# Grouped-query softmax attention on one core: per-head PV in the last twelve pairs, Q transposed as 4-byte words, V loaded five pairs behind K

## The chip, the core and the metric

The kernel runs on one core of a Trainium2 chip. A core has five engines, each with its own instruction stream: TensorE (PE, the matrix multiplier; PEld in the profile is its loading of weights), VectorE (DVE), ScalarE (ACT), GpSimd (POOL) and SyncE (SP, which here only issues transfers). Sixteen DMA engines move data between HBM and the on-chip memory SBUF; PE writes to a second on-chip memory, PSUM. The metric is device time in microseconds (us), the median of several runs. The profile is of one further execution.

## The reference, cut to what matters

```python
B, Hq, Hkv, Sq, Sk, D = 16, 32, 8, 16, 2048, 128      # bf16 inputs
k = jnp.repeat(k, 4, axis=1); v = jnp.repeat(v, 4, axis=1)
scores = jnp.einsum("bhqd,bhkd->bhqk", q, k) * D ** -0.5
p = softmax(scores, axis=-1)
return jnp.einsum("bhqk,bhkd->bhqd", p, v)
```

Four query heads with 16 positions each share one K and one V of 2048 x 128, so that each of the 16 x 8 = 128 (batch, KV head) groups has 64 query rows.

## The kernel before

**Pairs.** Two groups make a pair, p = 0 to 63: 128 query rows on the 128 partitions, head 0 on rows 0 to 63 and head 1 on rows 64 to 127. A pair needs 1 MB of K and 1 MB of V. All loops are unrolled; each engine runs its list of operations in program order, and semaphores tie the lists together.

**Transfers (SP, L166 to L210).** For t = 0, 1, ... SP issues K of pair t, the Q of eight pairs where one is due (256 KB), V of pair t - VLAG, and the store of the output of pair t - 12 (32 KB). K has 6 buffers: K of pair p waits until VectorE has transposed K of p - 6 (L171). V has 8 buffers: V of p waits until PE is done with V of p - 8 (L177). V of the last pair, 63, comes as two halves, each with its own semaphore (L182 to L185). All go through one queue and are carried out in the order of issue.

**One pair's way through the engines:**

- VectorE transposes K of the pair in two instructions (L308, function kt). They move blocks of 4-byte words, so that two neighbouring bf16 stay together; the two of a word (called e) lie at a stride of 4 bytes afterwards. The 128 elements of a head are thus handled as four quarters of 32: half b, parity e.
- PE multiplies Q with K (the "S" operation, L261 and L217): 32 matmuls over 32 rows and 512 columns, four of them side by side, into the four PSUM banks S_ps. One S_ps serves all pairs, so S of pair p + 1 waits until VectorE has read S of pair p (L245).
- VectorE scales S into Sneg in SBUF and takes the row minimum of the negated scores (L324).
- ScalarE takes the exponential into P, in bf16, with the row sums (L354). P is laid out so that pairs of bf16 make 4-byte words.
- PE transposes P as 4-byte words, 8 transposes of 128 x 128 in two halves ("PT", L273) into two of three PSUM staging banks ST_ps; ScalarE copies each half to PT in SBUF (L364). In what follows this is called a copy of P.
- PE multiplies P with V ("PV"), three pairs late (PVLAG): for pairs 0 to 60 as 16 matmuls with 128 weight columns, both heads' P, against 256 columns, both heads' V (L289). Half of the result, one head's P with the other's V, is not used. For the last three pairs as 32 matmuls with 64 weight columns against 128 (L295), one for each head, into columns of S_ps that are free by then. The loop over j (16 blocks of 128 keys) is the same in both.
- ScalarE divides by the row sums and writes the output tile ("norm"): two instructions for pairs 0 to 60, since the two useful quarters of O_ps lie apart (L377), one for the last three (L381). PV of the next pair waits for it, as O_ps is used by all (L283); the last three wait for S of pair 63 having been read instead (L281).

**Q.** GpSimd copies the Q of eight pairs (a chunk, c = 0 to 7) into Q4 with each half of a row four times, once for each group of 32 partitions (L161). Then come four "Q parts" (i = 0 to 3) for each chunk: PE transposes into a staging bank ("QT", L239), ScalarE copies it to QT in SBUF ("qe", L344). Before the change, part i is the quarter (b, e): 8 transposes of bf16 at a stride of 4 bytes, 128 columns each. The parts of chunk 0 come at the start; those of chunk c + 1 come in the pairs p with p mod 8 = 2 to 5 of chunk c, one in each, after PT (L125 to L127). So 28 pairs carry a Q part, the last of them pair 53; the document calls them Q pairs.

**The order.** It is written out by hand (L115 to L137). In round p PE does S(p + 1), PV(p - 3), PT(p), and QT in a Q pair. ScalarE does exp(p), norm(p - 3), the two copies of P, and qe in a Q pair. VectorE does Sneg(p), the reciprocal of the row sums of p - 1, and the transposes of K of p + 2. At the end PE does, after S(63): PV(59), PT(62), PV(60), PV(61), PV(62), PT(63), PV(63). ScalarE does, after exp(62): norm(59), the copies of P of 62, exp(63), norm(60), norm(61), norm(62), the copies of P of 63, norm(63).

Of the kernel before, what the change touches and what calls it, by code (L numbers as in the profile page):

```python
# [5 lines left out]
ACT = mybir.ActivationFunctionType  # L6
# [9 lines left out]
NO = 8  # L16
NQ = 2
NSTAGE = 3
VLAG = 4
PVLAG = 3  # L20
SLAG = 12
QLEAD = 7


def bass_standalone__gqa_softmax__sampling_kernel(
# [26 lines left out]
    KT = [sb(f"KT{i}", [128, 2 * J * 64], F32) for i in range(NKT)]  # L52
    Qn = [sb(f"Qn{i}", [128, 8, 128], BF16) for i in range(NQ)]
    Q4 = sb("Q4", [128, 8, 2, 4, 64], BF16)
    QT = [sb(f"QT{i}", [128, 4, 1024], BF16) for i in range(2)]
    Sneg = [sb(f"Sneg{i}", [128, Sk], F32) for i in range(2)]
    P = [sb(f"P{i}", [128, Sk // 2], F32) for i in range(2)]
    PT = [sb(f"PT{i}", [128, J // 2, 128], F32) for i in range(NPT)]
# [83 lines left out]
        return ST_ps[:, 512 * (u % NSTAGE):512 * (u % NSTAGE + 1)]  # L142

    def o_ap(p):
        x = p - (NP - 3)
        return S_ps[:, 512 * x:512 * x + 128]

    with nc.Block() as block:
# [63 lines left out]
        @block.tensor  # L212
        def _(pe):
            pe.wait_ge(sem_id, 3)

            def matmul_on_loaded(out, lhsT, rhs, tile, start, stop):
                return pe.add_instruction(mybir.InstMatmult(  # L217
                    name=nc.get_next_instruction_name(), engine=mybir.EngineType.PE,
                    ins=[pe.lower_ap(rhs), pe.lower_ap(lhsT, for_matmul_weights=True)],
                    outs=[pe.lower_ap(out)],  # L220
                    start_tensor_calc=start, stop_tensor_calc=stop,
                    tile_size=(32, 64), tile_position=tile, ldweights=False,
                ))

            def free(u):
                if u >= NSTAGE:
                    pe.wait_ge(sem_ev, u - NSTAGE + 1)

            for op in pe_prog:
                if op[0] == "QT":  # L230
                    _, c, i, u = op
                    if i == 0:
                        pe.wait_ge(sem_q4, c + 1)
                    free(u)
                    dst = stage_ap(u).bitcast(BF16)
                    src = Q4[:, :, :, :, :].rearrange("p j b r (c e) -> p j b e (r c)", e=2)
                    b, e = divmod(i, 2)
                    for j in range(8):
                        ins = pe.transpose(dst[:, 128 * j:128 * (j + 1)], src[:, j, b, e, :], ident[:, :])  # L239
                    ins.then_inc(sem_st, 1)  # L240
                elif op[0] == "S":
                    _, p = op
                    pe.wait_ge(sem_kt, 2 * p + 2)
                    if p >= 1:
                        pe.wait_ge(sem_max, p)  # L245
                    c, i = divmod(p, 8)
                    if i == 0:
                        pe.wait_ge(sem_ev, last_q[c, 3] + 1)
                    kt = KT[p % NKT][:, :].bitcast(BF16).rearrange("p (t b y e) -> p b e t y", t=J // 2, b=2, e=2)
                    qt = QT[c % 2]  # L250
                    for acc in range(4):
                        b, e = divmod(acc, 2)
                        for u in range(2):
                            for r in range(4):
                                rows = slice(32 * r, 32 * (r + 1))
                                g, h = divmod(r, 2)
                                s_ap = S_ps[64 * g:64 * (g + 1), 512 * (2 * h + u):512 * (2 * h + u + 1)]
                                w = qt[rows, acc, 128 * i + 64 * g:128 * i + 64 * (g + 1)]
                                x = kt[rows, b, e, 4 * u:4 * (u + 1), :]
                                if u == 0:  # L260
                                    ins = pe.matmul(s_ap, w, x, start=(acc == 0), stop=(acc == 3))  # L261
                                else:
                                    ins = matmul_on_loaded(s_ap, w, x, (32 * r, 64 * g), acc == 0, acc == 3)
                    ins.then_inc(sem_s, 1)
                elif op[0] == "PT":
                    _, p, h, u = op
                    if h == 0:
                        pe.wait_ge(sem_exp, p + 1)
                    free(u)
                    dst = stage_ap(u)  # L270
                    for t in range(4):
                        x = 4 * h + t
                        ins = pe.transpose(dst[:, 128 * t:128 * (t + 1)], P[p % 2][:, 128 * x:128 * (x + 1)], ident4[:, :])  # L273
                    ins.then_inc(sem_st, 1)
                elif op[0] == "PV":
                    _, p = op
                    pe.wait_ge(sem_ev, last_p[p, 1] + 1)
                    if p < NP - 1:
                        pe.wait_ge(sem_v[p % NV], 16 * (p // NV + 1))
                    if p >= NP - 3:  # L280
                        pe.wait_ge(sem_max, NP)  # L281
                    elif p >= 1:
                        pe.wait_ge(sem_nm, p)  # L283
                    pt = PT[p % NPT][:, :, :].bitcast(BF16).rearrange("p t (q e) -> p t e q", e=2)
                    for j in range(J):
                        if p == NP - 1 and j % 8 == 0:
                            pe.wait_ge(sem_vl[j // 8], 16)
                        if p < NP - 3:
                            ins = pe.matmul(  # L289
                                O_ps[:, 0:256], pt[:, j // 2, j % 2, :], Vb[p % NV][:, :, j, :],  # L290
                                start=(j == 0), stop=(j == J - 1),
                            )
                            continue
                        for g in range(2):
                            ins = pe.matmul(  # L295
                                o_ap(p)[64 * g:64 * (g + 1), :],
                                pt[:, j // 2, j % 2, 64 * g:64 * (g + 1)],
                                Vb[p % NV][:, g, j, :],
                                start=(j == 0), stop=(j == J - 1),
                                skip_group_check=True,  # L300
                            )
                    ins.then_inc(sem_pv, 1)
# [34 lines left out]
        def _(act):  # L337
            for op in act_prog:
                if op[0] == "qe":
                    _, c, i, u = op  # L340
                    act.wait_ge(sem_st, u + 1)
                    if c >= 2 and i == 0:
                        act.wait_ge(sem_s, 8 * (c - 1))
                    act.activation(  # L344
                        QT[c % 2][:, i, :].rearrange("p (a j) -> p a j", j=8),
                        stage_ap(u).bitcast(BF16).rearrange("p (j a) -> p a j", j=8), ACT.Copy,
                    ).then_inc(sem_ev, 1)
                elif op[0] == "exp":
                    _, p = op
                    act.wait_ge(sem_max, p + 1)  # L350
                    if p >= 2:
                        act.wait_ge(sem_st, last_p[p - 2, 1] + 1)

                    act.activation(  # L354
                        P[p % 2][:, :].bitcast(BF16).rearrange("p (n y e) -> p n y e", n=16, e=2),
                        Sneg[p % 2][:, :].rearrange("p (n e y) -> p n y e", n=16, e=2), ACT.Exp,
                        bias=nbias[:, p:p + 1], scale=-1.0, accum_out=rowsum[:, p:p + 1],
                    ).then_inc(sem_exp, 1)
                elif op[0] == "pe":
                    _, p, h, u = op  # L360
                    act.wait_ge(sem_st, u + 1)
                    if h == 0 and p >= NPT:
                        act.wait_ge(sem_pv, p - NPT + 1)
                    act.activation(  # L364
                        PT[p % NPT][:, 4 * h:4 * (h + 1), :].rearrange("p t q -> p (t q)"),
                        stage_ap(u), ACT.Copy,
                    ).then_inc(sem_ev, 1)
                else:
                    _, p = op
                    act.wait_ge(sem_pv, p + 1)  # L370
                    act.wait_ge(sem_rec, p + 1)
                    if p >= NO:
                        act.wait_ge(sem_o[p % NO], 16 * (p // NO))
                    if p < NP - 3:
                        for g in range(2):
                            rows = slice(64 * g, 64 * (g + 1))
                            ins = act.activation(Osb[p % NO][rows, :], O_ps[rows, 128 * g:128 * (g + 1)], ACT.Copy,  # L377
                                                 scale=rrec[rows, p:p + 1])
                        ins.then_inc(sem_nm, 1)
                        continue  # L380
                    act.activation(Osb[p % NO][:, :], o_ap(p), ACT.Copy,  # L381
                                   scale=rrec[:, p:p + 1]).then_inc(sem_nm, 1)
# [28 lines left out]
```

## Time and profile before

| | |
|---|---|
| time, median of 3 runs (lowest, highest) | 348.14 us (347.62, 348.2) |
| the profiled execution: its own time | 348.5 us |
| its span, first to last instruction | 346.7 us |
| PE, ACT, DVE busy | 93%, 89%, 86% of the span |
| moved | 138.94 MB, 401 GB/s over the span |
| granted TensorE clock, mean | 0.995 |

The profile's page has the busy share of each engine, the span in 40 slices (8.67 us each here), the chain of work that ended last, and groups of instructions: line, engine, operation, output and inputs, shape, count, then busy time, mean ns of one, and the idle time ahead of them with what ended it. Besides the page, the trace answers with a timeline of instructions (start, us, engine, line), with who waited for whom, and with the time from the issue of a transfer to its landing. A matmul's busy time holds its way through the array; how fast matmuls follow each other is read from their starts. Times below are counted from the start of the span.

### The profile page before, as it was taken

The page shows a single profiled execution, that of the slowest core. Times are in us where ns is not written, and L with a number is a line of the kernel's source. Part 1 is how long each engine was busy: PE and PEld are TensorE (multiplying, and loading weights), DVE is VectorE, ACT ScalarE, POOL GpSimd, SP SyncE. Part 2 cuts the span into 40 slices and gives each one's busy share as a digit, 9 for nine tenths or more (in the row PEclk, how much of TensorE's full clock was granted, in tenths as well). Part 3 has the DMA queues.
Part 4 walks back from the last instruction along what each step waited for, and adds up shares of the span by engine and source line. Part 5 has one row for each costly group of instructions (what it writes and reads, how often), then busy time and mean ns, then how long its engine had stood idle before and what let it go on. Part 6 is the DMA issues. An engine that isn't in the chain of part 4 may idle for free.

```text
span 346.7 us, 8194 instructions
## 1 busy us (share of the span) xinstructions
PE 323.0 (93%) x3888; PEld 196.1 (57%) x2864; DVE 297.2 (86%) x320; ACT 308.7 (89%) x414; POOL 30.3 (9%) x15
## 2 busy tenths in 40 slices
PE   0667999999999999999999999999999999999995
PEld 0423565556555655665655565566566556555564
DVE  2279988998899989998989988999899989899950
ACT  1438999999999999999999999999999999999995
POOL 4500003000300004000040003000040000000000
PEclk9989999999999999999999999999999999999999
DMA  7999999999999999999999999999999999999981
GB/s 297 425 421 414 409 416 412 413 418 416 412 419 414 416 416 414 416 419 420 410 415 416 419 416 413 418 416 416 413 418 415 418 413 417 417 416 416 412 320 31
DMA packets 37300, 138.94 MB, mean 401 GB/s; under 512 B 11408, under 2 KB 11408, under 8 KB 29072
## 3 DMA queue, kind: packets, MB, share of 16 engines
q1 hardware_dynamic: 37264, 138.42, 98.6%
q8 instruction: 27, 0.44, 0.5%
q14 instruction: 9, 0.07, 0.1%
HBM read 136.31 MB, written 2.10 MB: 399 GB/s over the span
## 4 chain that ended last, share of the span: by engine, by line
PE 67%; ACT 21%; issue 6%; DVE 2%; DMA 2%; POOL 1%; ACTq 0%; SPq 0%
PE O_ps L289 25%; PE S_ps L261 15%; PE ST_ps L273 13%; PE S_ps L217 13%; ACT P L354 11%; ACT QT L344 5%; ACT PT L364 3%; PE ST_ps L239 2%; ACT O L377 2%; DMA Qn<-in_q_dram 2%; DVE KT L308 1%; POOL Q L161 1%; DVE Sneg L324 1%; PE S_ps L295 0%; ACT O L381 0%
## 5 line engine op out<-in xcount | busy, mean ns | idle before, releaser
L324 DVE TENSOR_SCALAR_CACHE_REDUCE Sneg<-S_ps 128x2048 f32<-128x2048 f32 x64 | 146.6, 2290 | 33.1 <-PE S_ps L217 32.0
L354 ACT ACTIVATE P<-Sneg,nbias 128x2048 bf16<-128x2048 f32 x64 | 158.7, 2479 | 7.7 <-DVE Sneg L324 6.1
L308 DVE STREAM_TRANSPOSE KT<-Kn 128x1024 f32<-128x1024 f32 x128 | 150.6, 1216 | 6.6 <-DMA Kn<-in_k_dram 6.6
L289 PEld LDWEIGHTS O_ps<-Vb,PT 128*128 128x128 bf16 x976 | 90.6, 98 | 49.2 <-issue 21.8
L289 PE MATMUL O_ps<-Vb,PT 128*128 128x256 bf16 x976 | 117.2, 273 | 0.0
L261 PE MATMUL S_ps<-KT,QT 32*64 32x512 bf16 x1024 | 103.5, 392 | 5.8 <-DVE Sneg L324 4.4
L217 PE MATMUL S_ps<-KT,QT 32*64 32x512 bf16 x1024 | 102.2, 387 | 0.0
L364 ACT ACTIVATE PT<-ST_ps 128x512 f32<-128x512 f32 x128 | 69.6, 595 | 5.1 <-PE ST_ps L273 3.0
L273 PE MATMUL ST_ps<-ident,P 128*128 128x128 f32 x512 | 69.9, 280 | 4.0 <-ACT P L354 2.9
L261 PEld LDWEIGHTS S_ps<-KT,QT 32*64 32x64 bf16 x1024 | 29.6, 103 | 69.0 <-issue 57.3
L273 PEld LDWEIGHTS ST_ps<-ident,P 128*128 128x128 f32 x512 | 55.9, 142 | 17.6 <-ACT P L354 16.4
L377 ACT ACTIVATE O<-O_ps,rrec 64x128 bf16<-64x128 f32 x122 | 44.1, 361 | 11.7 <-PE O_ps L289 10.1
L161 POOL COPY Q<-Qn 128x4096 bf16<-128x4096 bf16 x8 | 28.8, 3600 | 226.9 <-PE ST_ps L239 222.6
L344 ACT ACTIVATE QT<-ST_ps 128x1024 bf16<-128x1024 bf16 x32 | 32.7, 1032 | 9.3 <-PE ST_ps L239 9.3
L239 PE MATMUL ST_ps<-ident,Q 128*128 128x128 bf16 x256 | 20.6, 231 | 10.2 <-POOL Q L161 10.2
L239 PEld LDWEIGHTS ST_ps<-ident,Q 128*128 128x128 bf16 x256 | 18.2, 104 | 10.5 <-issue 10.2
L315 DVE RECIPROCAL rrec<-rowsum 128x1 f32<-128x1 f32 x64 | 10.1, 158 | 3.9 <-ACT P L354 3.9
L354 ACT ACTIVATION_READ_ACCUMULATOR P<-Sneg,nbias 128x1 f32 x64 | 12.1, 189 | 0.0
L324 DVE DVE_READ_ACCUMULATOR Sneg<-S_ps 128x1 f32 x64 | 5.3, 83 | 0.0
L295 PE MATMUL S_ps<-Vb,PT 128*64 128x128 bf16 x96 | 3.1, 220 | 1.0 <-ACT PT L364 1.0
L295 PEld LDWEIGHTS S_ps<-Vb,PT 128*64 128x64 bf16 x96 | 2.7, 110 | 1.5 <-ACT PT L364 1.3
L381 ACT ACTIVATE O<-S_ps,rrec 128x128 bf16<-128x128 f32 x3 | 1.0, 365 | 1.2 <-PE S_ps L295 1.2
(8 smaller groups left out, 3.0 us busy)
## 6 DMA issues: line engine op xcount, KB each, us to landing
Kn<-in_k_dram SPq DMA_DIRECT2D x64, 1024.0 KB, 16.0
Vb<-in_v_dram SPq DMA_DIRECT2D x63, 1024.0 KB, 17.9
Qn<-in_q_dram SPq DMA_DIRECT2D x8, 256.0 KB, 15.5
out_dram<-O SPq DMA_DIRECT2D x64, 32.0 KB, 15.9
Vb<-in_v_dram SPq DMA_DIRECT2D x2, 512.0 KB, 12.3
```

Source lines behind the costliest of these rows:

```text
L161: gp.tensor_copy(Q4[:, :, :, :, :].rearrange("p j b r x -> p (j b) r x"), src.unsqueeze(2).to_broadcast([128, 16, 4, 64]),).then_inc(sem_q ...
L217: return pe.add_instruction(mybir.InstMatmult(name=nc.get_next_instruction_name(), engine=mybir.EngineType.PE, ins=[pe.lower_ap(rhs), pe.l ...
L239: ins = pe.transpose(dst[:, 128 * j:128 * (j + 1)], src[:, j, b, e, :], ident[:, :])
L261: ins = pe.matmul(s_ap, w, x, start=(acc == 0), stop=(acc == 3))
L273: ins = pe.transpose(dst[:, 128 * t:128 * (t + 1)], P[p % 2][:, 128 * x:128 * (x + 1)], ident4[:, :])
L289: ins = pe.matmul(O_ps[:, 0:256], pt[:, j // 2, j % 2, :], Vb[p % NV][:, :, j, :], start=(j == 0), stop=(j == J - 1),)
L308: dve.transpose(KT[p % NKT][:, :].rearrange("p (t b e a x) -> p x e t b a", t=J // 2, b=2, e=2, x=2)[:, x, :, :, :, :], Kn[p % NK][:, :].b ...
L324: dve.tensor_scalar(Sneg[p % 2][:, :].rearrange("p (t h x) -> p h t x", t=8, h=2), S_ps[:, :].rearrange("p (h t x) -> p h t x", t=8, h=2), ...
L344: act.activation(QT[c % 2][:, i, :].rearrange("p (a j) -> p a j", j=8), stage_ap(u).bitcast(BF16).rearrange("p (j a) -> p a j", j=8), ACT. ...
L354: act.activation(P[p % 2][:, :].bitcast(BF16).rearrange("p (n y e) -> p n y e", n=16, e=2), Sneg[p % 2][:, :].rearrange("p (n e y) -> p n ...
L364: act.activation(PT[p % NPT][:, 4 * h:4 * (h + 1), :].rearrange("p t q -> p (t q)"), stage_ap(u), ACT.Copy,).then_inc(sem_ev, 1)
L377: ins = act.activation(Osb[p % NO][rows, :], O_ps[rows, 128 * g:128 * (g + 1)], ACT.Copy, scale=rrec[rows, p:p + 1])
```

## The change

Three edits. VLAG goes from 4 to 5: V of pair t - 5 is issued behind K of pair t. The Q parts become (half b, half x of the eight pairs): 4 transposes of 4-byte words instead of 8 of bf16, one copy of 128 x 512 4-byte words instead of 128 x 1024 bf16; QT then holds words, and S reads its weights from it at a stride of 4 bytes. And the form of PV with 32 narrow matmuls and one norm instruction starts at pair NP - 12 = 52 instead of 61; pairs 52 to 60 write it to O_ps, the last three to S_ps as before.

```diff
-VLAG = 4
+VLAG = 5
+NFAST = 12
...
-    QT = [sb(f"QT{i}", [128, 4, 1024], BF16) for i in range(2)]
+    QT = [sb(f"QT{i}", [128, 2, 1024], F32) for i in range(2)]
...
     def o_ap(p):
+        if p < NP - 3:
+            return O_ps[:, 0:128]
...
-                    dst = stage_ap(u).bitcast(BF16)
-                    src = Q4[:, :, :, :, :].rearrange("p j b r (c e) -> p j b e (r c)", e=2)
-                    b, e = divmod(i, 2)
-                    for j in range(8):
-                        ins = pe.transpose(dst[:, 128 * j:128 * (j + 1)], src[:, j, b, e, :], ident[:, :])
+                    dst = stage_ap(u)
+                    src = Q4[:, :, :, :, :].bitcast(F32).rearrange("p j b r c -> p j b (r c)")
+                    b, x = divmod(i, 2)
+                    for j in range(4):
+                        ins = pe.transpose(dst[:, 128 * j:128 * (j + 1)], src[:, 4 * x + j, b, :], ident4[:, :])
...
-                    qt = QT[c % 2]
+                    qt = QT[c % 2][:, :, :].bitcast(BF16).rearrange("p b (n e) -> p b e n", e=2)
...
-                                w = qt[rows, acc, 128 * i + 64 * g:128 * i + 64 * (g + 1)]
+                                w = qt[rows, b, e, 128 * i + 64 * g:128 * i + 64 * (g + 1)]
...
-                        if p < NP - 3:
+                        if p < NP - NFAST:
                             ins = pe.matmul(
                                 O_ps[:, 0:256], pt[:, j // 2, j % 2, :], Vb[p % NV][:, :, j, :],
...
-                        QT[c % 2][:, i, :].rearrange("p (a j) -> p a j", j=8),
-                        stage_ap(u).bitcast(BF16).rearrange("p (j a) -> p a j", j=8), ACT.Copy,
+                        QT[c % 2][:, i // 2, :].rearrange("p (a x j) -> p x a j", x=2, j=4)[:, i % 2],
+                        stage_ap(u).rearrange("p (j a) -> p a j", j=4), ACT.Copy,
...
-                    if p < NP - 3:
+                    if p < NP - NFAST:
                         for g in range(2):
```

## The prediction

> **What bounds the kernel now.** I read the span in slices first, then the waits, then the landings of single transfers beside the timeline.
>
> The page's line of DMA shares is full from the second slice to the 38th:
>
> ```profile
> DMA  7999999999999999999999999999999999999981
> ```
>
> The busy time by stretches gives a DMA share of 1.02 to 1.03 at 412 to 418 GB/s in every stretch from 10 to 330 us. The one queue carries transfers in the order of issue, so the last V lands at a fixed time, whatever the engines do. But the list of waits holds almost no wait for data:
>
> ```profile
> POOL Q L161 <- PE ST_ps L239: 222.6, 7, 37.0
> ...
> DVE KT L308 <- DMA Kn<-in_k_dram: 6.6, 2, 5.8
> POOL Q L161 <- DMA Qn<-in_q_dram: 4.3, 1, 4.3
> ```
>
> K is waited for twice, at the start; V never. So the engines are the slower side, running on a lead of loaded data. I took the lead for K pair by pair, as the start of its transpose on VectorE less its landing: 13.7 us for pair 4, 10.3 for 24, 4.9 for 48, 2.1 for 62, 0.59 for 63. For V (start of PV less landing): 17.5 for pair 4, 12.7 for 24, 8.3 for 48, 5.1 for 59, 2.9 for 62. The lead melts because eight pairs take 40.5 us of computing (VectorE's Sneg of pair 32 starts at 180.01, of 40 at 220.50) and a little more of transfers (K of 32 lands at 164.06, of 40 at 205.38: 41.3). Both sides finish together: **a faster computation gains only until it meets the DMA.**
>
> The engines themselves, per pair. Without a Q part the period is 4.65 to 4.76, and three engines are full at once. VectorE: Sneg 2.21 to its accumulator read, then 0.08, then two K transposes 2.35, 4.66 with gaps. PE, by starts: S 1.93, PV 1.76, PT 0.96, sum 4.65. ScalarE: exp 2.57, norm 0.74, two copies of P 1.08, 4.4 plus waits. With a Q part the four periods are 5.2, 5.56, 5.34 and 5.42: ScalarE adds the copy of Q and is full.
>
> The end of the trace, ScalarE's timeline:
>
> ```profile
> 338.06 2.47 ACT L354 ACTIVATE P<-Sneg,nbias 128x2048 bf16<-128x2048 f32 x1
> 340.44 0.19 ACT L354 ACTIVATION_READ_ACCUMULATOR P<-Sneg,nbias 128x1 f32 x1
> 340.54 0.72 ACT L377 ACTIVATE O<-O_ps,rrec 64x128 bf16<-64x128 f32 x2
> 341.28 0.63 ACT L381 ACTIVATE O<-S_ps,rrec 128x128 bf16<-128x128 f32 x2
> 341.80 1.08 ACT L364 ACTIVATE PT<-ST_ps 128x512 f32<-128x512 f32 x2
> 344.06 0.37 ACT L381 ACTIVATE O<-S_ps,rrec 128x128 bf16<-128x128 f32 x1 [1.18 <-PE S_ps L295]
> ```
>
> The last exponential is late by queueing on ScalarE, not for data. PV(63) runs 342.94 to 344.04, and from its start to the end of the span is 3.74 us. The data were there: V of 62 landed at 336.97 (issue 323.72 plus 13.25), the halves of 63 at 338.30 and 339.62.
>
> **The change part by part.** Rows of the page:
>
> ```profile
> L289 PE MATMUL O_ps<-Vb,PT 128*128 128x256 bf16 x976 | 117.2, 273 | 0.0
> L364 ACT ACTIVATE PT<-ST_ps 128x512 f32<-128x512 f32 x128 | 69.6, 595 | 5.1 <-PE ST_ps L273 3.0
> ...
> L273 PE MATMUL ST_ps<-ident,P 128*128 128x128 f32 x512 | 69.9, 280 | 4.0 <-ACT P L354 2.9
> ...
> L344 ACT ACTIVATE QT<-ST_ps 128x1024 bf16<-128x1024 bf16 x32 | 32.7, 1032 | 9.3 <-PE ST_ps L239 9.3
> ```
>
> *Q as words.* The copy of Q is 1032 ns now; the same number of words as a copy of P (L364) is 595. The new copy reads and writes with strides; so does L344, and 1032 for 1024 elements against 595 for 512 is a line through 0.16 us with no mark of strides. Bounds 0.6 and 1.03; I take 0.6, saving 0.43 on ScalarE. On PE, 8 bf16 transposes hold up the next S by 0.54 (196.70 to 197.24). Four of words are half of a PT, half of 0.96: 0.48. So in a Q pair PE needs 4.65 + 0.48 = 5.13, ScalarE about 5.38 - 0.43 = 4.95, VectorE 4.66: the period becomes 5.13 instead of 5.38, **0.25 us x 28 = 7 us** of computing time, with PE next in line. Bounds: nothing (the copy stays 1.03) and 12 us (0.43 x 28). S reads its weights at a 4-byte stride, as PV does: L289's weight loads of 128 x 128 at that stride take 98 ns, S's 32 x 64 now 103; I count nothing. In the start, four parts are bound by ScalarE's 3.78 us; PE at half pace needs about as long, so at most some 0.5 us, which only lengthens the lead.
>
> *Narrow PV.* In the last pair 32 narrow matmuls take 1.10 us (342.94 to 344.04); 16 wide ones take 1.85. That is 0.75 less on PE, and one norm of 0.37 instead of 0.74, for nine pairs. While VectorE needs 4.66 a pair these are hidden, a saving of 4.70 - 4.66 a pair, under 0.5 us in all. In the end game they count once each: norm(59) ahead of exp(63), and norm(60) behind it: 0.74 us. The Trainium skill (TensorEngine Tiling (Array Packing), Restrictions) says that column tiling switches off fast weight load, which speaks against this edit: narrow weight loads should then be dearer. The rows show 110 ns against 98 and yet the 1.10 us above; by the rule alone one would expect a loss, and here the trace decides.
>
> *V five pairs behind.* K of pair p moves one V transfer forward, some 2.55 us; V of p moves one K back, except for the last five, which come last either way. K of 63 takes the place of V of 58, which landed at 305.47 + 18.6 = 324.05, instead of 309.58 + 17.1 = 326.64. SP's waits: K of t waits for the transpose of t - 6, and V behind it in the queue waits with it. The dangerous one is K of 8, issued at 23.45 after standing for pair 2's transpose: what is issued ahead of it lasts until 34.72 now, until 32.2 with one V less, 8.7 us of cover. If that cover were gone, each us would go straight into the end. Later on transfers are issued 12 to 21 us ahead of their landing. I count nothing.
>
> **The sum.** By pair 51 the Q pairs have given 6.5 us or more, so K's lead, 3.7 plus 2.55, is used up, and V's, 9.1 less 2.55, too. From there the DMA sets the pace at some 5.1 us a pair; the narrow PV keeps PE at 3.9 of it. The last pairs, with landings taken from the trace: K(63) 324.05, transposed 326.4; Sneg(62) to 328.7. V(58) 326.64, PV(58) to 327.75, PT(61), copies to 329.5, exp(62) to 332.2. S(63) 328.9 to 330.8, Sneg(63) to 333.2. PT(62) 332.3, copies to 334.1, exp(63) to 336.75. PV(60) and PV(61) are done by 335.5, and then PE stands for V(62): 336.97. In program order behind it: PV(62) 1.03 + 0.05, PT(63) from 338.05. Its first half is copied 0.70 after its start (28.98 to 29.68 in the second pair), two copies 1.08, 0.05 to PE: PV(63) at 339.88, its second half of V there since 339.62. That is 3.06 us earlier than 342.94. exp(63) has 1.3 us to spare. So the span becomes 346.7 - 3.1 = 343.6, the profiled time 348.5 - 3.1 = 345.4. The median of the runs shown is 0.36 below the profiled execution: **345.1**.
>
> **The rivals.**
>
> *The computation stays the bound* (12%): the Q part gains little, because the strided copy stays near 1.03 or the transposes of words cost PE more. Then the tail's 0.74 and 0.45 of the narrow PV remain: 348.14 - 1.2 = 346.9. For it: Q pairs have three engines close together. Against: the lead over exp(63) needs only 2.1 us, a third of the 7.
>
> *The clock drops* (6%): PE now idles between transfers. In the trace PE stood from 18.8 to 21.3 and the stretch 22.43 to 25.85 had a granted clock of 0.50, while stretches with 0.9 to 1.1 us idle of 3.41 kept 1.00. The new gap is 1.5 us ahead of PV(62). PT at half clock took 1.97 instead of 1.09, so the last chain would lose about 2.5: 347.6. The Trainium skill (TensorE: Matmul & The Clock Gate, Why this matters for your kernels) warns only of gaps over about 3 us; by that figure nothing would happen, yet the 2.5 us gap here was enough.
>
> *One fetch of code less in the way* (6%): 27 fetches of 16 KB take about 1.05 us each on the same DMA engines. The last landing is that of the slowest engine; should one fetch slip past it, 344.0.
>
> *The Q part is dearer than today* (8%), the one on the other side: place, the 28 copies on ScalarE or transposes on PE; if the strides of 4-byte words double the copy to 1.19, each Q pair grows by 0.16, 28 x 0.16 = 4.5, less 1.2: 351.4. It decides from 0.07 us a part (0.07 x 28 = 1.9, less 1.2, is 0.7). Against: L344 shows no cost of strides.
>
> **How the numbers follow.** The forecast, DMA-bound at the end, has 68%. The range 344.0 to 347.3 takes in the missed fetch and the compute-bound case, 86% in all. I take 0.2%, 0.7 us, as what a measurement of this kernel can tell from no change: faster 0.68 + 0.12 + 0.06 = 0.86, same 0.06 (the clock), slower 0.08.
>
> **What would show it.** Right: copies of Q near 600 ns; Q pairs near 5.1 us; from pair 51 or so waits of VectorE for K and of PE for V; K(63) near 324 and V(62) near 337; PE idle ahead of PV(62). Wrong: K's lead still positive at the end, a clock under 1 in the last 30 us, a DMA share under 1 before 330 us, or V(62) landing elsewhere than 337.

## The result, and the profile after

| | before | changed |
|---|---|---|
| time, median (lowest, highest) | 347.88 us (347.54, 348.20), 4 runs | 345.77 us (345.50, 346.02), 4 runs |
| profiled execution: time, span | 348.5, 346.7 us | 346.02, 344.1 us |
| K of 63 landed; its transpose began | 326.64; 327.23 | 323.15; 323.18 |
| exp(63) began, ended | 338.06, 340.54 | 334.08, 336.54 |
| V of 62 landed; PV(62) began | 336.97; 339.83 | 337.44; 337.52 |
| PV(63) began | 342.94 | 340.37 |
| last half of V of 63 landed | 339.62 | 340.09 |

The ratio is 0.9939, 95% interval 0.9922 to 0.9957: about 2.1 us less, between 1.5 and 2.7. The forecast was 3.0 less (345.1 from 348.14).

The waits of the changed kernel (who waited for whom, us in total, times, longest):

```profile
PEld O_ps L298 <- issue: 12.7, 9, 3.0
...
DVE KT L311 <- DMA Kn<-in_k_dram: 9.4, 7, 5.7
...
PE O_ps L298 <- issue: 7.0, 6, 2.3
```

VectorE stands for K seven times instead of twice. The transposes of K of 63, before and after, show it at the end:

```profile
327.23 2.35 DVE L308 STREAM_TRANSPOSE KT<-Kn 128x1024 f32<-128x1024 f32 x2
```

```profile
323.18 2.37 DVE L311 STREAM_TRANSPOSE KT<-Kn 128x1024 f32<-128x1024 f32 x2 [0.48 <-DMA Kn<-in_k_dram]
```

PE's waits for V carry the name "issue", as the view ties no transfer to them. The landings tell: from pair 47 on every PV but those of 59 and 60 starts within 0.4 us of the landing of its V, for pair 63 of the last half (pair 56: 315.30 and 315.39), where V of pair 56 had 7.45 us of lead before.

The transposes and copies of Q on the page (before, they were 256 transposes of bf16 in L239 and copies of 1032 ns in L344):

```profile
L242 PE MATMUL ST_ps<-ident,Q 128*128 128x128 f32 x128 | 20.4, 291 | 10.1 <-POOL Q L164 10.1
L347 ACT ACTIVATE QT<-ST_ps 128x512 f32<-128x512 f32 x32 | 19.3, 603 | 10.0 <-PE ST_ps L242 10.0
```

And the end on the timeline, PE and ScalarE, from the wait for V of 62:

```profile
337.52 1.08 PE L298 MATMUL S_ps<-Vb,PT 128*64 128x128 bf16 x32 [1.55 <-issue]
...
338.54 1.09 PE L276 MATMUL ST_ps<-ident,P 128*128 128x128 f32 x8
...
339.23 1.08 ACT L367 ACTIVATE PT<-ST_ps 128x512 f32<-128x512 f32 x2 [0.22 <-PE ST_ps L276]
...
340.37 1.09 PE L298 MATMUL S_ps<-Vb,PT 128*64 128x128 bf16 x32 [0.74 <-ACT PT L367]
```

PE is idle for 1.55 us, does PV(62) when V of 62 has landed, then the transposes of pair 63, whose P has been ready since 336.54; then the copies and PV(63). This is the chain of the forecast.

### The profile page after: what moved, and what is told of

Read it like the earlier page. It is cut to its first block, busy times and chain, and to the rows that moved or that the text cites. A ratio compares the mean times of both kernels' runs of the same rounds, so it can differ in the third digit from the quotient of the medians.

```text
span 344.1 us, 8217 instructions
## 1 busy us (share of the span) xinstructions
PE 314.5 (91%) x3904; PEld 189.9 (55%) x2880; DVE 297.4 (86%) x320; ACT 292.3 (85%) x405; POOL 30.3 (9%) x15
## 4 chain that ended last, share of the span: by engine, by line
PE 87%; issue 5%; ACT 3%; DVE 2%; DMA 2%; POOL 1%; SPq 0%; ACTq 0%
PE O_ps L292 28%; PE S_ps L264 18%; PE ST_ps L276 16%; PE S_ps L220 16%; PE ST_ps L242 4%; PE O_ps L298 2%; DMA Qn<-in_q_dram 2%; ACT P L357 1%; DVE KT L311 1%; POOL Q L164 1%; DVE Sneg L327 1%; PE S_ps L298 1%; ACT PT L367 1%; ACT QT L347 0%; ACT O L380 0%
## 5 line engine op out<-in xcount | busy, mean ns | idle before, releaser
L292 PEld LDWEIGHTS O_ps<-Vb,PT 128*128 128x128 bf16 x832 | 77.2, 98 | 42.3 <-issue 34.1
L292 PE MATMUL O_ps<-Vb,PT 128*128 128x256 bf16 x832 | 99.9, 273 | 0.0
L380 ACT ACTIVATE O<-O_ps,rrec 64x128 bf16<-64x128 f32 x104 | 37.7, 363 | 14.2 <-PE O_ps L292 13.4
L242 PE MATMUL ST_ps<-ident,Q 128*128 128x128 f32 x128 | 20.4, 291 | 10.1 <-POOL Q L164 10.1
L347 ACT ACTIVATE QT<-ST_ps 128x512 f32<-128x512 f32 x32 | 19.3, 603 | 10.0 <-PE ST_ps L242 10.0
L242 PEld LDWEIGHTS ST_ps<-ident,Q 128*128 128x128 f32 x128 | 16.4, 151 | 10.1 <-issue 10.1
L298 PE MATMUL O_ps<-Vb,PT 128*64 128x128 bf16 x288 | 9.8, 220 | 7.0 <-issue 7.0
L298 PEld LDWEIGHTS O_ps<-Vb,PT 128*64 128x64 bf16 x288 | 8.5, 110 | 12.7 <-issue 12.7
L384 ACT ACTIVATE O<-O_ps,rrec 128x128 bf16<-128x128 f32 x9 | 3.3, 367 | 6.7 <-PE O_ps L298 6.7
## 6 DMA issues: line engine op xcount, KB each, us to landing
Qn<-in_q_dram SPq DMA_DIRECT2D x8, 256.0 KB, 15.2
```

The costliest lines, as they stand in the source:

```text
L242: ins = pe.transpose(dst[:, 128 * j:128 * (j + 1)], src[:, 4 * x + j, b, :], ident4[:, :])
L292: ins = pe.matmul(O_ps[:, 0:256], pt[:, j // 2, j % 2, :], Vb[p % NV][:, :, j, :], start=(j == 0), stop=(j == J - 1),)
L298: ins = pe.matmul(o_ap(p)[64 * g:64 * (g + 1), :], pt[:, j // 2, j % 2, 64 * g:64 * (g + 1)], Vb[p % NV][:, g, j, :], start=(j == 0), stop ...
```

## The experiments

The theory: in the changed kernel the DMA sets the end, through V of 62 and what stands behind it in program order; in the kernel before it was the engines. The main rival: the saved engine time itself is the gain. All kernels were timed in five rounds against the kernel before, each beside runs of it on the same chip. They were timed in three groups, on three chips, so small differences between kernels of different groups are better read from the ratios than from the medians.

### Each edit alone, and each pair of edits

The diffs are single constants or the edits of the change. V later alone (the diff), and Q as words alone (the changed kernel with VLAG = 4 and NFAST = 3):

```diff
-VLAG = 4
+VLAG = 5
```

> Only the order of V is changed, on the kernel before. Theory (the engines set the end of the kernel before, the DMA that of the changed one): no change, 347.9, since the kernel before waits for no data after its start; K's lead at pair 63 grows from 0.6 to about 3.1 us and V's at pair 59 falls from 5.1 to about 2.5, both unused. Rival (the order of V is what brought the gain): 346 or less.

> Only Q as words. Theory: Q pairs at 5.15 us, but K of 63 still lands near 326.6, 0.6 us ahead of where its transpose began before, and the last pairs keep the wide PV; a gain of 0.6 to 0.9, 347.1, with VectorE waiting for K from about pair 48 on. Rival (the sum of saved engine time counts): 7 us less, 341.

The narrow PV alone, and the change without Q's edit (narrow PV and V later):

```diff
+NFAST = 12
...
-                        if p < NP - 3:
+                        if p < NP - NFAST:
...
```

> Only the narrow PV from pair 52 on. Theory: the engines stay the bound; one norm instruction less ahead of the last exponential and one behind it, 0.74, and up to 0.45 where VectorE was not quite full: 346.7 to 347.2. Rival (PE's 0.75 a pair counts in full for nine pairs): 341.

> The changed kernel with Q in bf16 as before (V later and narrow PV alone). Theory: the engines stay the bound, as in the narrow PV alone, 346.7, with K's lead at the end still 2 us or more. Rival (Q's edit adds nothing, the end game is all): 345.8, as the changed kernel.

The changed kernel with one constant set back, V's order or the narrow PV:

```diff
-VLAG = 5
+VLAG = 4
```

> The changed kernel with V four pairs behind K as before. Theory: K of 63 lands 2.5 us later, near 326; the last exponential then ends near 338.4, just when PV(62), which stands for V of 62 at about 337.4, is through: 345.8 to 346.4, so the order of V is worth 0 to 0.6. Rival (the whole gain hangs on K's earlier landing): 347 or more.

```diff
-NFAST = 12
+NFAST = 3
```

> The changed kernel with the wide PV up to pair 60. Theory: each wide PV behind its V costs 0.75 more at the end, the last exponential ends near 338.0 and PV(62) runs 0.4 later: 346.2. Rival (narrow PV matters only as saved engine time that the DMA swallows): 345.8, no loss.

| kernel | median us | ratio to before (95%) | K's lead at 63 | exp(63) began | V of 62 landed | PV(62) | PV(63) |
|---|---|---|---|---|---|---|---|
| before | 347.8 to 347.9 | 1 | 0.59 | 338.06 | 336.97 | 339.83 | 342.94 |
| V later alone | 347.42 | 0.9978 (0.9961 to 0.9994) | 2.96 | 338.07 | 337.20 | 339.83 | 342.93 |
| Q as words alone | 346.58 | 0.9954 (0.9941 to 0.9967) | 0.02 | 336.02 | 337.06 | 337.78 | 340.88 |
| narrow PV alone | 346.02 | 0.9941 (0.9926 to 0.9955) | 0.15 | 335.86 | 336.94 | 337.03 | 340.31 |
| V later, narrow PV | 346.06 | 0.9944 (0.9928 to 0.9961) | 2.12 | 335.91 | 337.43 | 337.52 | 340.56 |
| Q as words, narrow PV | 346.04 | 0.9947 (0.9929 to 0.9965) | 0.02 | 336.01 | 337.02 | 337.18 | 340.45 |
| Q as words, V later | 345.43 | 0.9923 (0.9909 to 0.9937) | 0.02 | 334.19 | 337.06 | 337.15 | 340.00 |
| all three (the change) | 345.77 | 0.9939 (0.9922 to 0.9957) | 0.03 | 334.08 | 337.44 | 337.52 | 340.37 |

The columns after the ratio are of the profiled execution. The gains don't add up: the narrow PV alone brings nearly all of the change, and Q and V's order together bring all of it. Wherever two edits meet, PV(62) starts within 0.2 us of the landing of V of 62. This is a floor, and there are several ways to it. In the three kernels that have the narrow PV but not both other edits, exp(63) ends at 338.3 to 338.5 and PV(62) at 338.2 to 338.8. With the narrow PV alone, and with Q as words and the narrow PV, the transposes of pair 63 wait for P (338.33 and 338.48, against PV(62) at 338.19 and 338.40); with V later and the narrow PV they wait for PV(62) (338.80, against 338.37). So there the engines and the DMA bind within 0.5 us of each other. V later with the narrow PV was expected at 346.7 and came to 346.06, for the reason that follows.

*Narrow PV alone* gained 1.9 where 0.7 to 1.2 was expected. Its timeline of ScalarE, from exp(62) to exp(63), and Sneg(63) on VectorE, before and there:

```profile
331.32 2.50 ACT L357 ACTIVATE P<-Sneg,nbias 128x2048 bf16<-128x2048 f32 x1
...
334.31 0.37 ACT L384 ACTIVATE O<-O_ps,rrec 128x128 bf16<-128x128 f32 x1 [0.40 <-PE O_ps L298]
334.89 1.09 ACT L367 ACTIVATE PT<-ST_ps 128x512 f32<-128x512 f32 x2 [0.21 <-PE ST_ps L276]
335.86 2.47 ACT L357 ACTIVATE P<-Sneg,nbias 128x2048 bf16<-128x2048 f32 x1
```

```profile
334.34 2.29 DVE L324 TENSOR_SCALAR_CACHE_REDUCE Sneg<-S_ps 128x2048 f32<-128x2048 f32 x1 [2.29 <-PE S_ps L217]
```

```profile
333.29 2.29 DVE L327 TENSOR_SCALAR_CACHE_REDUCE Sneg<-S_ps 128x2048 f32<-128x2048 f32 x1 [2.11 <-PE S_ps L220]
```

In the kernel before exp(63) begins 1.43 us after Sneg(63) is done (334.34 + 2.29 = 336.63, then 338.06). It is the same 1.43 us in every round from pair 55 on: ScalarE stands behind PV and runs late, though VectorE is on time. With the narrow PV this shrinks from pair 56 on, and at pair 63 it is 0.28 (333.29 + 2.29 = 335.58, then 335.86). So 1.15 us of the backlog are gone. Sneg(63) is 1.05 earlier besides, as VectorE's rounds take 4.53 from pair 58 on instead of 4.65 to 4.76. Together exp(63) is 2.20 earlier, and with one short norm instead of a long one behind it PV(63) is 2.63 earlier.

*Q as words alone* shows the cap of K. The waits of VectorE for K there:

```profile
DVE KT L311 <- DMA Kn<-in_k_dram: 14.8, 20, 5.6
```

Twenty waits instead of two: VectorE is at K's landing from pair 46 on, and what the Q pairs had given was waited away again (Sneg of pair 40 is 4.4 us earlier than before, of 52 3.3, of 63 only 2.1). It gained 1.3; 0.6 to 0.9 was expected, and K of 63 landed 1.1 earlier than I took.

*Without the narrow PV* the time did not rise by 0.4, as I expected, but is 0.3 lower, with intervals that overlap. exp(63) ended at 336.67, 0.4 ahead of V of 62 and 1.5 ahead of the transposes that need it (338.17). So on top of the other two edits the narrow PV brings nothing.

### The DMA as the bound

This kernel leaves out the V of head 1 in pairs 0 to 51, half of the work of each wide PV; it serves to measure time alone.

```diff
-                                O_ps[:, 0:256], pt[:, j // 2, j % 2, :], Vb[p % NV][:, :, j, :],
+                                O_ps[:, 0:128], pt[:, j // 2, j % 2, :], Vb[p % NV][:, 0, j, :],
...
```

> The changed kernel with the wide PV of pairs 0 to 51 cut to the V of head 0 (128 columns instead of 256; the outputs of head 1 in these pairs are P of head 1 with V of head 0). Same number of instructions and transfers, about 0.9 us less of PE in each of 52 pairs. Theory (the DMA sets the end): the same time, 345.8 within 0.4, with V waited for from an earlier pair on. Rival (PE still sets the end): 2 us less or more.

345.61 us, ratio 0.9928 (0.9914 to 0.9943), against 345.77 of the change. K's lead is used up by pair 31 (0.02 us) instead of 53, PV(62) starts at 337.15 behind V of 62 at 337.06. Sneg of pair 32 begins 7.5 us earlier than in the change (169.09 and 176.56; 1.0 of it is there at pair 2 already), and nothing of it that can be told from zero is left at the end: in the changed kernel the DMA sets the end.

### What V's order is worth

V later alone was expected to change nothing. Its median is 0.5 lower, and its twelve runs lie between 346.07 and 348.52. The kernel before is narrower below: none of the runs beside it is under 347.69. The profiled run of V later alone is at its slow end, 348.5, and shows nothing but K's lead. The start differs between executions: Sneg of pair 2 begins at 28.90 in the trace of the changed kernel and at 25.95 in that of the kernel with the reordered end (below), whose programs are the same up to PV(61). So I made the start of the engines earlier. In the kernel before PE runs S(0) at half pace (four matmuls side by side every 0.43 us from 15.2 to 18.1, every 0.22 later; the granted clock reads 1.00 there), and the end of S(1) and the first transposes of P at a granted clock of 0.50 (22.43 to 25.85).

```diff
+            def idle(n):
+                for _ in range(n):
+                    pe.transpose(O_ps[:, 256:384], ident4[:, :], ident4[:, :])
+
+            idle(36)
             for op in pe_prog:
...
                     ins.then_inc(sem_s, 1)
+                    if p == 0:
+                        idle(16)
```

> The kernel before with idle transposes on PE into unused columns of O_ps: 36 ahead of the first Q part, 16 behind S(0), so that S(0) and S(1) do not run at half clock. Theory (the kernel before is set by the engines, and the spread of the run with V later alone comes from how much of its start falls into half clock): the engines arrive some 1.5 to 2 us earlier, but K of 63 lands at 326.6, 0.6 before its transpose began, so the gain stops at 0.6 to 0.9: 347.0 to 347.3. Rival (the spread comes from the transfers): 347.9, no change.

> The same idle transposes with V five pairs behind K. Theory: K of 63 lands 2.5 us earlier, so the 1.5 to 2 us are gained in full: 346.0 to 346.4, the lower end of the run with V later alone, and with a spread under 0.8 instead of its 2.45. Rival: 347.4, with the spread as wide as before.

With V four pairs behind: 347.58 us, ratio 0.9989 (0.9979 to 1.0), less gain than expected. With V five pairs behind: 345.91, ratio 0.9948 (0.9934 to 0.9962). The idle transposes did not bring all of S(0) to full pace: its matmuls still come every 0.43 us up to 17.0 in the first trace, and at the end of S(0) in the other; S(1) and the first transposes of P are at full pace. By the medians the 52 instructions alone are worth 0.2 us, V's order alone 0.5, and both together 1.8 (0.4, 0.8 and 1.8 by the ratios). The engines are ahead of the kernel before by about as much with either order (Sneg of pair 32 at 178.38 and 177.96, against 180.01). But with V four pairs behind, K of 63 lands at 326.56 and its transpose starts at 326.58, no lead left; with five it lands at 324.11, with 1.06 us to spare at 325.17. So the kernel before stood within 0.6 us of a second bound, the landing of K, and V's order moves that landing 2.5 earlier. With V five pairs behind the spread was not under 0.8, as I had expected, but 1.15 (345.65 to 346.80, five runs). So that the scatter of V later alone comes from the start fits the different starts above, but is not shown.

### The narrow PV everywhere

```diff
-NFAST = 12
+NFAST = 64
```

> The changed kernel with the narrow PV in all pairs: 52 pairs more with 32 matmuls instead of 16, 1664 PE instructions more, 0.75 us of PE less in each. Theory (the DMA sets the end; fetches of code run on the same DMA engines, and the slowest of them sets the last landing): no gain from the engines; some 6 or 7 fetches of 16 KB more, of which one or none meets the slowest engine: V of 63 lands 0.4 to 1.1 later, 346.2 to 346.9. Rival (more engine time saved, more gained): under 345.4.

346.58 us, ratio 0.9975 (0.9956 to 0.9993): slower than the change, as expected. The trace shows two things, of which I had only the first. The last half of V landed at 341.26 instead of 340.09. Of its sixteen completion marks (the steps in which its semaphore rises to 16) the last eight came at 339.24 to 341.26 instead of 338.18 to 340.09 (mean of all sixteen 337.13 instead of 336.78). The page counts 33 fetches of code instead of 27; that these made the landing late is my explanation and not shown. And PE, idle more often, was put to half clock three times after the start; the last time at the end. The busy time by stretches (stretch; us; busy us and count of PE, PEld, DVE, ACT, POOL; granted clock; DMA share; GB/s) and the timeline:

```profile
334.30:337.70 3.40, 1.50 (x47) 1.35 (x47) 0.16 (x1) 2.67 (x4) 0.00 (x0) 0.99 0.62 233
337.70:341.10 3.40, 3.20 (x34) 2.62 (x28) 0.00 (x0) 1.13 (x3) 0.00 (x0) 0.51 0.45 139
```

```profile
337.33 1.66 PE L298 MATMUL S_ps<-Vb,PT 128*64 128x128 bf16 x32 [1.54 <-issue]
...
338.93 1.97 PE L276 MATMUL ST_ps<-ident,P 128*128 128x128 f32 x8
```

PV(62) took 1.66 instead of 1.08 and the transposes of 63 took 1.97 instead of 1.09, and PV(63) began at 341.58, later than in the change although V of 62 was there 0.2 earlier. The clock is not the whole of it: the seven runs with a mean granted clock of 0.99 or more took 346.27 to 346.62 us, still more than the slowest run of the change (346.02); the five runs with less took 347.14 to 349.46.

### A shorter chain behind V of 62

The transposes and copies of pair 63 go ahead of PV(62) and norm(62), in the changed kernel and in the one with the wide PV up to pair 60 (NFAST = 3):

```diff
+    transposes(NP - 1)
     pv(NP - 2)
     norm(NP - 2)
-    transposes(NP - 1)
     pv(NP - 1)
```

> The changed kernel with the transposes of P of pair 63 ahead of PV(62) on PE, and the copies of P of 63 ahead of norm(62) on ScalarE. Theory (the end is V of 62, then PV(62), then the transposes and copies of pair 63 in program order): these no longer stand behind V of 62; PV(63) ends 0.55 us behind the last half of V at 340.1, 0.7 earlier than now: 345.1. Rival (the last exponential or the copies bind): 345.8, the same.

> The reordered end (transposes of P of 63 ahead of PV(62)) with the wide PV up to pair 60. Theory: V of 63 lands some 0.2 to 0.4 earlier with one fetch of code less, and the last exponential still ends ahead of V of 62: 344.6 to 345.0, the fastest so far or equal to it. Rival (without the narrow PV the engines bind once the end no longer stands behind V of 62): 345.4 or more.

344.94 us, ratio 0.991 (0.9894 to 0.9925), and 344.89, ratio 0.9914 (0.9901 to 0.9927): the fastest kernels of the study, and equal. The timeline of the first:

```profile
337.50 1.09 PE L276 MATMUL ST_ps<-ident,P 128*128 128x128 f32 x8 [1.27 <-ACT P L357]
...
338.53 2.04 PE L298 MATMUL S_ps<-Vb,PT 128*64 128x128 bf16 x64
...
340.61 0.37 ACT L384 ACTIVATE O<-S_ps,rrec 128x128 bf16<-128x128 f32 x1 [0.59 <-PE S_ps L298]
```

PV(62) and PV(63) run without a gap and end 0.68 us behind the last half of V (339.89). The last norm is at 340.61 instead of 341.50.

## Why the prediction was right or wrong

- **The bound moves to the DMA.** Right, and by the mechanism that was forecast: the thin PV gains nothing, and the chain of the end is the forecast's (exp(63) ended at 336.54 where 336.75 was forecast, and PE stood idle ahead of PV(62)).
- **The size.** 3.06 us were forecast for PV(63), 2.57 measured in the profiles. From the landing of V of 62 to PV(63) the forecast had 2.91 us; it took 2.93. The term that was mis-sized is the landing: 337.44 instead of 336.97. The first completion mark of the last half of V came at the same time as before (333.59, before 333.56), the last one 0.47 later. In the traces of all kernels but the one with narrow PV everywhere the last landing lies between 339.38 and 340.17, with 26 to 28 fetches of code, and the number of fetches does not order them. So "the last V lands at a fixed time" holds to about 0.8 us from trace to trace; which packets make the difference stays open. Most of the rest of the miss is the choice of execution: the profiled ones differ by 2.48 us (348.5 and 346.02), the medians by 2.11, as the profiled execution of the kernel before lay 0.62 above its median.
- **Q as words.** Right: the copy takes 603 ns, eight pairs 39.5 us (Sneg of 32 to 40: 176.56 to 216.05) instead of 40.5. The lead ran out somewhat before "by pair 51" on V's side, at 47, and somewhat after it on K's, at 53.
- **The narrow PV.** "In the end game they count once each: 0.74" failed, and with it the price of the first rival, 346.9: the narrow PV alone reached 346.02, and with V later 346.06. Two readings were wrong. The sum left out the 1.43 us by which ScalarE ran behind VectorE in every round: PE's order S, PV, PT puts the transposes of P behind the PV, and the next exponential behind their copies, and a shorter PV and norm took 1.15 us of this away. And VectorE was not full at 4.66 a pair: its rounds went down to 4.53, which made Sneg(63) 1.05 earlier where "under 0.5 us in all" was counted. That the forecast did not suffer is because exp(63) had 1.3 us to spare in it. By the run without the narrow PV, 345.43, this edit was not needed for the result at all.
- **V five pairs behind.** "I count nothing" held for stalls: K of pair 8 was issued at 22.83, 9.7 us before the V queued ahead of it landed (32.50). But the edit lifts the cap that K's landing put on the kernel before, worth up to 1.7 us to whoever has engine time to gain (347.58 against 345.91 with the idle transposes). By the lead of 0.59 us this could have been read off the trace.
- **The rivals.** The clock did not drop in the end of the changed kernel's profile; it did in the kernel with narrow PV everywhere, and there PT took the 1.97 us that the rival named; PV(63) came 1.4 us later than by the 2.93 behind V of 62 (337.24), where the rival had put 2.5. A dearer Q part did not come, and no slower kernel.
- **A reading of the rates.** The stretches from 10 to 330 us moved 409 to 421 GB/s, not 412 to 418; nothing in the sum rests on it.

## What to carry to other kernels

Ahead of a change to an engine, write down for some pairs how long each tile has been waiting for its user: a lead that melts towards zero says that the DMA is the next bound, and where. Behind that point gains don't add up: here several edits reached the same floor, and only a shorter chain from the last landings to the end brought more. An engine that is always the same time late against its producer holds a backlog: here a shorter link of its round gave most of it (1.15 of 1.43 us) back, once, at the end.

## What the runs showed of the hardware

A transfer's parts end far apart under a full queue: the sixteen completion marks of the last half of V, taken here as one for each DMA engine, came between 333.59 and 340.09 us in the changed kernel, with a mean of 336.78. Were they even, some 3 us would be left to gain; this is an estimate from these numbers, and it wasn't tried.

The half clock needs less than a long pause. In the kernel with the reordered end PE stood still for 1.98 us ahead of PV(58), in a stretch of 3.41 us with 1.43 us of PE work, and the next 3.42 us ran at a clock of 0.50. exp(63) ended 0.8 later there than in the changed kernel (337.36), but the end lost at most 0.1 us: this execution took 345.01, and the other three, at a mean clock of 1.00, took 344.89 to 344.98. The Trainium skill (TensorE: Matmul & The Clock Gate, Why this matters for your kernels) warns of gaps over about 3 us; here the shorter gap was enough. But the length of the gap does not decide alone: in the changed kernel PE stood still for 2.34 us ahead of PV(58), across two stretches of the clock's records, the emptier with 1.77 us of PE work, and the clock stayed at 1.00. In the fourteen traces, cut from 10 us on into stretches of 3.41 us in step with the records of the clock, all thirty stretches with at most 1.5 us of PE work were followed by one at 0.50 (fourteen of them at the end of the run), and none with 1.6 or more was. The busy time by stretches, with the reordered end and then in the changed kernel:

```profile
324.09:327.50 3.41, 1.43 (x41) 0.82 (x31) 3.41 (x3) 1.80 (x2) 0.00 (x0) 1.00 1.03 401
327.50:330.92 3.42, 3.42 (x31) 2.06 (x21) 0.27 (x3) 2.02 (x4) 0.00 (x0) 0.50 1.04 414
```

```profile
322.99:326.40 3.41, 1.77 (x32) 0.41 (x12) 3.22 (x3) 2.97 (x4) 0.00 (x0) 1.00 1.03 405
326.40:329.81 3.41, 2.71 (x52) 2.03 (x48) 1.41 (x3) 1.37 (x4) 0.00 (x0) 1.00 1.03 410
```
